# Attention scores: from two split products per head to one fp32 product of two heads side by side

## The chip, the cores and the metric

The kernel runs on one core of one Trainium2 chip. The metric is device time in microseconds (us) from the first to the last instruction of a launch, as the median over runs. Before the change it is 1330.2 us (three runs, 1329.62 to 1331.72). Engines are called as in the profile: PE is the matmul engine (PEld its weight loads), DVE the vector engine, ACT the scalar engine, POOL GpSimd, SP the engine that issues the DMAs.

## The reference

Three stages run one after the other. Shapes: q, k and v are (4, 8, 576, 64), that is 4 batches, 8 heads, 576 positions and 64 numbers per head.

```python
scores = (1.0 / np.sqrt(D)) * np.matmul(q, k.transpose(0, 1, 3, 2))
kth = np.partition(scores, -32, axis=-1)[..., -32:-31]
scores = np.where(scores >= kth, scores, -1e9)
attn = np.exp(scores - scores.max(-1, keepdims=True))
attn = attn / (attn.sum(-1, keepdims=True) + 1e-09)
x = np.matmul(attn, v)             # then heads side by side: (2304, 512)
x = ((x @ w_a) * (x @ w_b)) @ w_out
# each token goes to one of 8 experts (argmax of its cosine to expert_emb):
out[mask] = gate_w[mask, None] * (np.maximum(x[mask] @ w1[e], 0.0) @ w2[e])
```

The change touches only the first line, the scores. What is chosen after them (the 32 largest of a row, later one expert of eight) is sensitive to rounding, which is why scores are computed to fp32 precision and not in one product of rounded operands.

## The kernel before, in words

Attention works on *row tiles*: 128 query positions of one head against all 576 keys. There are 144 of them. A *part* is one pair of heads (`pr`) of a batch, and in it a share of the queries: A and B are 256 queries each, T the last 64. The list `SEQ` (0A 0BT 1A 1BT 2A 2BT 3AT 3B) gives the order of the parts, each for four pairs of heads, so 32 parts. A part has two row tiles per head, four in all, and where it has a T a fifth (kind 2), which holds 64 queries of either head. The first part of a batch and pair is its *lead*: it loads and turns the keys and stores them in DRAM, and the batch's other part reads them back.

How one row tile goes through the engines:

- **Load and split** (`load_q`, `load_k`, `split_k`, `split_qk`, L223 to L294). Raw fp32 rows of q and k are split into a rounded part (hi, type fp32r) and a rest (lo). Except for the first part, POOL does it: two instructions for the keys of a lead, three for the queries of each part. In memory a head's 64 numbers of hi and of lo lie side by side, so that 128 numbers of a position make one column to turn.
- **Turn** (`turn_qk`, L296 to L344): PE turns 128x128 blocks (L307) into PSUM, ACT copies them out (L317, L325, L331, L341). Keys: [hi | lo] over the 128 rows. Queries: twice, as [hi | lo] and as [lo | hi].
- **Scores** (`scores`, L352 to L366): for a row tile and each half of the keys (288 columns) two fp32r matmuls over all 128 rows (L364): the hi-with-hi and lo-with-lo products come out of the first, the mixed ones out of the second. ACT copies the sum to SBUF (L365). For kind 2 it is four matmuls a half, from the padded tile `qm`.
- **Top 32** (`topk`, L368): DVE takes the eight largest four times (MAX8, L385) and strikes them out between (L388).
- **Softmax** (`softmax`, L392): ACT (L397), POOL (L400), ACT (L402).
- **Turn and mix** (`turn`, `mix`, `along`, L404 to L466): PE turns the weights (L419) five blocks a row tile, ACT copies them out (L422). After the last row tile of a part PE multiplies them with the values, both heads in the two column halves of the array (L460), and spreads the sums' reciprocals (L440).

Into this stream the second stage is woven as *background*: nine groups (`moe1`, L624) of 288 fp32r matmuls of 256 columns (L683) and 72 of 512 columns (L652), with ACT and POOL work behind each, and the routing of each 128 tokens (`route`, L711).

The order is written out by hand for PE, DVE, ACT and POOL. The loop at L864 makes one *step* per row tile: `topk` of row tile `step`, softmax of `step - 2`, turning of `step - 4`, scores of `step + AHEAD_Q`, and turning of q and k from `AHEAD_P` steps ahead (`flip_next`). L946 sets the order inside a step:

```python
for slot_, g in enumerate((tg, sg, tg, mg, sg)):
    if g is not none and not run(g) and g is mg and mixes:
```

`tg` turns, `sg` is the scores, `mg` the mix of the part that has just ended. So the first half of the keys is scored between the two turnings, and the second half at the end of the step, behind the mix. Each `run` of one of them (and of each piece of `flip_next`) is followed by background worth `share`, which is the step's time budget (`STEP`, 5.4 us) less the estimated PE time of its own work, divided by the number of pieces that are expected (L935 to L945). Each engine works through its own list in order: an instruction that waits holds up all behind it. PSUM buffers of name `tr` (four) are shared by turning, scores, mix and the weights' preparation. `s` (the scores of a row tile) has `SB` buffers.

Once the last row tile is done the remaining background runs alone (L1126), and then the experts.

Of the kernel before, what the change touches and what calls it, by code (L numbers as in the profile page):

```python
# [10 lines left out]
F32 = mybir.dt.float32  # L11
# [45 lines left out]
SB = 5  # L57
# [15 lines left out]
AHEAD_P = 5  # L73
AHEAD_Q = 2
# [8 lines left out]
def fused_kernel(  # L83
# [39 lines left out]
    kT_d = drm.tile([B * NP, P, 2 * S], F32, name="kT_d")  # L123
# [74 lines left out]
    with ExitStack() as ph:  # L198
# [9 lines left out]
        qms = [wk.tile([P, 2, 2, P], F32R, name=f"qm{i}", bufs=1) for i in range(QM)]  # L208
        for t in qms:
            dve.memset(t.bitcast(F32), 0.0)  # L210
# [12 lines left out]
        def load_q(o):  # L223
            r = wk.tile([P, 5, D], F32, name="qr")
            h0 = 2 * o.pr
            for h in range(2):
                if o.M:
                    sp.dma_start(
                        r[:, 2 * h : 2 * h + 2, :].rearrange("p c d -> p (c d)"),
                        q[o.b, h0 + h, 0:512, :].rearrange("(p c) d -> p c d", c=4)[:, o.c : o.c + 2, :].rearrange(  # L230
                            "p c d -> p (c d)"
                        ),
                    )
                if o.tail:
                    sp.dma_start(r[h * 64 : (h + 1) * 64, 4, :], q[o.b, h0 + h, 512:576, :])
            return r

        def load_k(o, b, pr):
            h0 = 2 * pr
            kr = wk.tile([P, 9, D], F32, name="kr", bufs=1)  # L240
            sp.dma_start(
                kr[:, 0:8, :].rearrange("p (h c) d -> p h (c d)", h=2),
                k[b, h0 : h0 + 2, 0:512, :].rearrange("h (p c) d -> p h (c d)", c=4),
            )
            for h in range(2):
                sp.dma_start(kr[h * 64 : (h + 1) * 64, 8, :], k[b, h0 + h, 512:576, :])
            o.kr = kr

        def split_k(o):
            kr = o.kr  # L250
            ks = wk.tile([P, 9, 2, D], F32R, name="ks", bufs=1)
            if o.n:
                yield from split(ks[:, :, 0, :], ks[:, :, 1, :], kr)
            else:
                act.activation(ks[:, :, 0, :], kr, AF.Copy)
                dve.tensor_tensor(ks[:, :, 1, :], kr, ks[:, :, 0, :].bitcast(F32), op=OP.subtract)
            o.ks = ks
# [13 lines left out]
        def prep(b, pr, part, n, c0):  # L271
# [11 lines left out]
            o.qs = None  # L283
            return o

        def split_qk(o):
            qr = o.qr
            if o.lead:
                yield from split_k(o)
            qs = wk.tile([P, 5, 3, D], F32R, name="qs", bufs=1)  # L290
            js = slice(0 if o.M else 4, 5 if o.tail else 4)
            yield from split(qs[:, js, 0, :], qs[:, js, 1, :], qr[:, js])
            pool.tensor_scalar(qs[:, js, 2, :], qr[:, js], 1.0, 1.0, op0=OP.mult, op1=OP.mult)
            o.qs = qs  # L294

        def turn_qk(o):  # L296
            qs = o.qs
            o.qT = wk.tile([P, 2, 512], F32R, name="qT")
            o.kT = wk.tile([P, 2, S], F32R, name="kT", bufs=2)
            if not o.lead:  # L300
                sp.dma_start(o.kT.bitcast(F32).rearrange("p h j -> p (h j)"), kT_d[o.b * NP + o.pr])
# [4 lines left out]
            def flip(pt, c, x):  # L306
                pe.transpose(pt[:, c * P : (c + 1) * P], x.rearrange("p a d -> p (a d)"), identr)  # L307

            if o.tail:
                o.qm = qms.pop(0)  # L310
                qms.append(o.qm)
                pt = ps.tile([P, 512], F32R, name="tr", bufs=NTR)
                for a in range(2):
                    flip(pt, a, qs[:, 4, a : a + 2, :])
                qv = pt.bitcast(F32)[:, : 2 * P].rearrange("p (a h j) -> p a h j", a=2, h=2)
                for h in range(2):
                    act.activation(o.qm[:, :, h, h * 64 : (h + 1) * 64], qv[:, :, h], AF.Copy)  # L317
                yield 0.11
            if o.lead:
                for h in range(2):  # L320
                    pt = ps.tile([P, 512], F32R, name="tr", bufs=NTR)
                    for c in range(4):
                        flip(pt, c, o.ks[:, h * 4 + c])
                    if h or o.n:
                        act.activation(o.kT[:, h, 0:512], pt.bitcast(F32), AF.Copy)  # L325
                    else:
                        dve.tensor_copy(o.kT[:, h, 0:512], pt.bitcast(F32))
                    yield 0.22
                pt = ps.tile([P, 512], F32R, name="tr", bufs=NTR)
                flip(pt, 0, o.ks[:, 8])  # L330
                act.activation(  # L331
                    o.kT[:, :, 512:576], pt.bitcast(F32)[:, 0:P].rearrange("p (h j) -> p h j", h=2), AF.Copy
                )
                sp.dma_start(kT_d[o.b * NP + o.pr], o.kT.bitcast(F32).rearrange("p h j -> p (h j)"))
                yield 0.06
            for a in range(2 if o.M else 0):
# [972 lines left out]
```

## Time and profile before

| | us |
|---|---|
| median of three runs | 1330.2 |
| profiled execution | 1327.13 |
| span of its trace | 1325.2 |
| PE busy | 1181.8 (89%) |
| DVE busy | 920.5 (69%) |
| ACT busy | 820.3 (62%) |
| POOL busy | 715.1 (54%) |

The profiled execution ran 3.1 us faster than the median; its time contains 1.9 us outside of the span. The shares are averages over three quite different stages: attention with background (until about 890 us), the remaining background alone (until about 1045 us), and the experts. Busy time of PE is the union of the recorded matmuls, which overlap one another; the time from one matmul's start to the next is shorter than the duration of one. "Granted clock" is the share of the TensorE clock of 2.4 GHz that was given in a stretch; it is either 1.0 or 0.5, so that a mean between them tells how much of the stretch was at 1.2 GHz.

### The profile page before, as it was taken

To read this page: it belongs to the slowest core of one execution; us is meant where nothing else is said; L and a number is where in the kernel's file an instruction comes from. 1 tells how busy PE (TensorE), PEld (TensorE's weight loads), DVE (VectorE), ACT (ScalarE), POOL (GpSimd) and SP (SyncE) were. 2 spreads that over 40 slices of the span, in tenths; PEclk is the share of its full clock that TensorE was granted. 3 is DMA by queue.
4 is the path that set the end of the run, shared out by engine and by line. 5 is a ranking of instruction groups with operands and counts; after the bars stand their busy time and mean duration, and the time that the engine had idled before them with its cause. 6 is when DMAs were issued, how large, how long until landed. Compare 5 with 4: busy or idle time off the path is not lost. (4 is left out here: it accounts for less than half of the span.)

```text
span 1325.2 us, 23082 instructions
## 1 busy us (share of the span) xinstructions
PE 1181.8 (89%) x7828; PEld 992.9 (75%) x7829; DVE 920.5 (69%) x1991; ACT 820.3 (62%) x1953; POOL 715.1 (54%) x1160
## 2 busy tenths in 40 slices
PE   4767878987999998999999998799999989999996
PEld 3444756666888787887887787678898868888885
DVE  6989999987899988998889899750100135444440
ACT  4776888876777777776778776663532335444441
POOL 4555767755676777765767766564455321111100
PEclk9786999897999999998999999799999999999999
DMA  6333476454666666665666656457998145555520
GB/s 210 121 103 124 143 244 210 177 179 146 182 184 223 185 208 193 212 180 176 204 183 192 202 165 203 146 170 247 331 300 246 40 129 197 174 168 173 176 91 19
DMA packets 125707, 237.00 MB, mean 179 GB/s; under 512 B 22765, under 2 KB 71021, under 8 KB 125586
## 3 DMA queue, kind: packets, MB, share of 16 engines
q1 hardware_dynamic: 121426, 225.20, 53.8%
q0 software_dynamic: 4160, 10.29, 2.4%
q8 instruction: 63, 1.03, 0.3%
q14 instruction: 58, 0.48, 0.1%
HBM read 195.38 MB, written 40.85 MB: 178 GB/s over the span
## 5 line engine op out<-in xcount | busy, mean ns | idle before, releaser
L385 DVE MAX8 t<-y 128x8 f32<-128x576 f32 x432 | 312.0, 750 | 3.1
L400 POOL TENSOR_TENSOR z<-s,z 128x576 f32<-128x576 f32 x144 | 206.2, 1432 | 105.6 <-ACT z L397 103.4
L683 PE MATMUL ab<-xg,wab 128*128 128x256 f32 x1440 | 215.8, 292 | 5.6 <-ACT gab L687 3.8
L388 DVE MATCH_REPLACE8 y<-t,y 128x576 f32<-128x576 f32 x288 | 214.0, 743 | 0.0
L683 PEld LDWEIGHTS ab<-xg,wab 128*128 128x128 f32 x1440 | 190.5, 193 | 9.0 <-ACT gab L687 4.4
L683 PE MATMUL ab<-raw,wab 128*128 128x256 f32 x1152 | 173.6, 292 | 6.8 <-ACT gab L687 4.4
L419 PE MATMUL tr<-ident,z 128*128 128x128 f32 x720 | 136.0, 289 | 44.5 <-ACT z L402 36.1
L402 ACT ACTIVATE z<-z,bi 128x576 f32<-128x576 f32 x144 | 111.6, 775 | 79.5 <-POOL z L400 79.4
L683 PEld LDWEIGHTS ab<-raw,wab 128*128 128x128 f32 x1152 | 152.4, 193 | 10.8 <-ACT gab L687 5.7
L385 DVE MAX8 t<-s 128x8 f32<-128x576 f32 x144 | 107.7, 748 | 54.1 <-ACT s L365 48.8
L364 PE MATMUL tr<-kT,qT 128*128 128x288 f32 x512 | 127.8, 334 | 18.1 <-ACT s L365 13.9
L422 ACT ACTIVATE wt<-tr 128x384 f32<-128x384 f32 (+2 forms) x320 | 127.4, 413 | 17.7 <-PE tr L419 16.9
L365 ACT ACTIVATE s<-tr 128x288 f32<-128x288 f32 x288 | 118.9, 413 | 30.0 <-PE tr L364 28.6
L419 PEld LDWEIGHTS tr<-ident,z 128*128 128x128 f32 x720 | 91.6, 147 | 60.2 <-ACT z L402 39.7
L652 PE MATMUL x<-wo,gh 128*128 128x512 f32 x432 | 135.6, 395 | 0.0
L1015 DVE TENSOR_TENSOR u<-raw,u 128x1024 fp32r<-128x1024 f32 x64 | 76.2, 1221 | 83.5 <-ACT u L1014 60.6
L1064 POOL DMA_INDIRECT out_dram<-o,ids x24 | 24.0, 1000 | 200.4 <-ACT o L1063 197.1
L1092 PE MATMUL y<-u,hT 128*128 128x512 f32 (+1 forms) x528 | 128.0, 396 | 0.4 <-DVE hT L1197 0.4
L639 POOL TENSOR_TENSOR gab<-gab 128x256 f32<-128x256 f32 x108 | 81.9, 758 | 84.7 <-ACT gab L687 79.5
L364 PEld LDWEIGHTS tr<-kT,qT 128*128 128x128 f32 x512 | 89.1, 205 | 32.1 <-ACT s L365 17.5
L397 ACT ACTIVATE z<-s,bi 128x576 f32<-128x576 f32 x144 | 112.7, 783 | 0.0
L1092 PEld LDWEIGHTS y<-u,hT 128*128 128x128 f32 (+1 forms) x528 | 89.7, 173 | 27.6 <-DVE hT L1197 0.5
(178 smaller groups left out, 2211.8 us busy)
## 6 DMA issues: line engine op xcount, KB each, us to landing
wab<-wab_d SPq DMA_DIRECT2D x192, 512.0 KB
raw<-in_moe_w_dram SPq DMA_DIRECT2D x28, 1024.0 KB
wab_d<-wab SPq DMA_DIRECT2D x24, 512.0 KB
kT_d<-kT SPq DMA_DIRECT2D x16, 576.0 KB
kT<-kT_d SPq DMA_DIRECT2D x16, 576.0 KB
vs<-in_v_dram SPq DMA_DIRECT2D x32, 256.0 KB
raw<-in_moe_w_a_dram SPq DMA_DIRECT2D x12, 512.0 KB
raw<-in_moe_w_b_dram SPq DMA_DIRECT2D x12, 512.0 KB
```

The lines of the kernel that those rows point to most:

```text
L364: pe.matmul(p, l, r, start=(i == 0), stop=(i == len(terms) - 1))
L365: act.activation(t.s[:, cs], p, AF.Copy, scale=SCALE)
L385: dve.max(v, cur)
L388: dve.match_replace(out=rest, in_to_replace=v, in_values=cur, imm_value=LOWEST)
L397: act.activation(t.w, t.s, AF.Relu, bias=t.bi[:, 1:2], scale=-HUGE)
L400: pool.tensor_tensor(t.w, t.s, t.w, op=OP.subtract)
L402: act.activation(t.w, t.w, AF.Exp, bias=t.bi[:, 0:1], accum_out=t.o.sm[:, t.slot : t.slot + 1])
L419: pe.transpose(pt[:, i * P : (i + 1) * P], t.w[:, k0 : k0 + P], ident)
L422: act.activation(th[:, sl, w], pv[:, :, src], AF.Copy)
L652: pe.matmul(px[t], g[:, ts], wo[:, w, f], start=(f == 0 and i == 0), stop=(f == NF - 1 and i == 2))
L683: pe.matmul(p[:, i], wt[:, a, c, :], xg[x][:, c, :], start=(j == 0), stop=(j == len(terms) - 1))
L1092: pe.matmul(p[:m], (hi, lo)[a], u[:, b, f % 4, :], start=(f == 0 and i == 0), stop=(f == NF2 - 1 and i == 2))
```

## The change

The splits go. Raw fp32 rows of both heads are loaded side by side, so that one 128x128 block holds the 64 numbers of head 0 and the 64 of head 1, and one turning serves both heads. The scores are one fp32 matmul over 64 rows per head and half of the keys: head 0 lies in rows 0 to 63 of the array and head 1 in rows 64 to 127, and the two matmuls stand next to each other in the program with outputs in two PSUM buffers. Row tiles change their order within a part to head 0, head 1, head 0, head 1. A pair's first half of the keys is scored in one step, the second half in the next. Kind 2 becomes one fp32 matmul over 128 rows a half, with the two heads' queries on the diagonal of `qm`. The scores come three row tiles ahead instead of two, the turning six instead of five, `s` has seven buffers instead of five and `kr` two instead of one. The kept copy of the turned keys in DRAM (`kT_d`) has half the size. The loads of q and k write and read 64 numbers (256 bytes) at a time.

```diff
-SB = 5
+SB = 7
...
-AHEAD_P = 5
-AHEAD_Q = 2
+AHEAD_P = 6
+AHEAD_Q = 3
...
-    kT_d = drm.tile([B * NP, P, 2 * S], F32, name="kT_d")
+    kT_d = drm.tile([B * NP, P, S], F32, name="kT_d")
...
         def load_k(o, b, pr):
             h0 = 2 * pr
-            kr = wk.tile([P, 9, D], F32, name="kr", bufs=1)
...
+            kr = wk.tile([P, 10, D], F32, name="kr", bufs=2)
             for h in range(2):
-                sp.dma_start(kr[h * 64 : (h + 1) * 64, 8, :], k[b, h0 + h, 512:576, :])
+                sp.dma_start(
+                    kr[:, 0:8, :].rearrange("p (c h) d -> p c h d", h=2)[:, :, h],
+                    k[b, h0 + h, 0:512, :].rearrange("(p c) d -> p c d", c=4),
+                )
+            sp.dma_start(kr[0:64, 8:10, :], k[b, h0 : h0 + 2, 512:576, :].rearrange("h s d -> s h d"))
             o.kr = kr
-
-        def split_k(o):
...
-        def split_qk(o):
...
         def turn_qk(o):
...
-            def flip(pt, c, x):
-                pe.transpose(pt[:, c * P : (c + 1) * P], x.rearrange("p a d -> p (a d)"), identr)
-
+            def flip(pt, at, x):
+                n = x.shape[0]
+                pe.transpose(pt[:, at : at + n], x.rearrange("p h d -> p (h d)"), ident[:n, :n])
+
+            if o.lead:
+                pt = ps.tile([P, 512], F32, name="tr", bufs=NTR)
+                for c in range(4):
+                    flip(pt, c * P, o.kr[:, 2 * c : 2 * c + 2, :])
...
+                yield 0.43
+            pt = ps.tile([P, 512], F32, name="tr", bufs=NTR)
+            for c in range(2 if o.M else 0):
+                flip(pt, c * P, o.qr[:, 2 * c : 2 * c + 2, :])
+            if o.tail:
+                flip(pt, o.M, o.qr[0:64, 4:6, :])
+            if o.lead:
+                flip(pt, 384, o.kr[0:64, 8:10, :])
...
-        def scores(t):
-            o = t.o
-            t.s = wk.tile([P, S], F32, name="s", bufs=SB)
-            for j in range(2):
-                p = ps.tile([P, 512], F32, name="tr", bufs=NTR)[:, :288]
+        def scores(i):
+
+            kind = rows[i][5]
+            o = live[i].o
+            if kind == 2:
+                tiles, js = [live[i]], range(2)
+            elif kind == 0:
+                tiles, js = [live[i], live[i + 1]], (0,)
+            else:
+                tiles, js = [live[i - 1], live[i]], (1,)
+            for j in js:
                 cs = slice(j * 288, (j + 1) * 288)
...
+                pt = [ps.tile([P, 512], F32, name="tr", bufs=NTR)[:, :288] for _ in tiles]
+                for h, t in enumerate(tiles):
+                    if kind == 2:
+                        pe.matmul(pt[0], o.qm, o.kT[:, cs], start=True, stop=True)
+                        continue
+                    hs, ts = slice(h * 64, (h + 1) * 64), slice(t.c * P, (t.c + 1) * P)
+                    pe.matmul(pt[h], o.qT[hs, ts], o.kT[hs, cs], start=True, stop=True)
+                for t, p in zip(tiles, pt):
+                    act.activation(t.s[:, cs], p, AF.Copy, scale=SCALE)
+                yield 0.48
...
-                A, Z, T = [(0, 0, 0), (0, 1, 1)], [(1, 0, 2), (1, 1, 3)], [(2, 0, 4)]
+                A, Z, T = [(0, 0, 0), (1, 0, 2)], [(0, 1, 1), (1, 1, 3)], [(2, 0, 4)]
...
-                cost, n = cost + (0.96 if live[step + AHEAD_Q].kind == 2 else 0.48), n + 2
+                k2 = live[step + AHEAD_Q].kind == 2
+                cost, n = cost + (0.96 if k2 else 0.48), n + 1 + k2
...
             if flips:
-                cost, n = cost + 0.44, n + 2
+                cost, n = cost + 0.44, n + 1
...
-            for _ in range(2):
-                flip_next()
+            flip_next()
```

How the order of the instructions changes is shown at one place of the program, around the mix that stands at 307 us in the trace before. On PE before, L364 is scores, L307 the turning of keys (`ks`) and queries (`qs`), L419 the turning of weights, L460 and L440 the mix and its sums, L683 and L730 background:

```order
408 L364 MATMUL tr<-kT,qT 128x288 x2
409 L307 MATMUL tr<-identr,ks 128x128 x8
410 L419 MATMUL tr<-ident,z 128x128 x3
411 L683 MATMUL ab<-raw_3366,wab 128x256 x4
412 L730 MATMUL ab<-enT,x1T 128x8 x4
413 L364 MATMUL tr<-kT,qT 128x288 x2
414 L419 MATMUL tr<-ident,z 128x128 x2
415 L460 MATMUL tr<-wt,vs 64x256 x10
416 L440 MATMUL tr<-ident,rc 64x128 x4
417 L364 MATMUL tr<-kT,qT 128x288 x2
418 L307 MATMUL tr<-identr,ks 128x128
```

On PE now, around the same mix (L342 is scores, L284 the turning of keys `kr` and queries `qr`, L398 of weights, L439 and L419 the mix, L662 and L709 background):

```order
356 L284 MATMUL tr<-ident,qr 128x128 x2
357 L284 MATMUL tr<-ident,kr 128x64
358 L398 MATMUL tr<-ident,z 128x128 x3
359 L342 MATMUL tr<-kT,qT 128x288 x2
360 L662 MATMUL ab<-raw_3059,wab 128x256 x4
361 L709 MATMUL ab<-enT,x1T 128x8 x4
362 L398 MATMUL tr<-ident,z 128x128 x2
363 L439 MATMUL tr<-wt,vs 64x256 x10
364 L419 MATMUL tr<-ident,rc 64x128 x4
365 L398 MATMUL tr<-ident,z 128x128 x3
366 L662 MATMUL ab<-raw_3057,wab 128x256 x4
367 L342 MATMUL tr<-kT,qT 128x288 x2
```

The half of a row tile's scores that stood behind the mix is gone from there: a step has one pair of score matmuls, and it stands between the two turnings, ahead of the mix.

On POOL before, just ahead of that place (L218 and L220 with `ks` and `qs` and L293 are the splits, L399 and L400 the softmax, L719 to L721 routing):

```order
226 L721 TENSOR_TENSOR st<-st,tau_95 128x1
227 L218 TENSOR_SCALAR ks<-kr 128x9x64
228 L399 TENSOR_SCALAR bi<-t_3167 128x1
229 L400 TENSOR_TENSOR z<-s,z 128x576
230 L220 TENSOR_TENSOR ks<-kr,ks 128x9x64
231 L218 TENSOR_SCALAR qs<-qr 128x4x64
232 L399 TENSOR_SCALAR bi<-t_3239 128x1
233 L400 TENSOR_TENSOR z<-s,z 128x576
234 L220 TENSOR_TENSOR qs<-qr,qs 128x4x64
235 L293 TENSOR_SCALAR qs<-qr 128x4x64
236 L399 TENSOR_SCALAR bi<-t_3294 128x1
237 L400 TENSOR_TENSOR z<-s,z 128x576
```

On POOL now at the same place (L378 and L379 are the softmax, L700 routing):

```order
182 L700 TENSOR_TENSOR st<-st,tau_95 128x1
183 L378 TENSOR_SCALAR bi<-t_2877 128x1
184 L379 TENSOR_TENSOR z<-s,z 128x576
185 L378 TENSOR_SCALAR bi<-t_2936 128x1
186 L379 TENSOR_TENSOR z<-s,z 128x576
187 L378 TENSOR_SCALAR bi<-t_2988 128x1
188 L379 TENSOR_TENSOR z<-s,z 128x576
```

The five splits are gone and nothing takes their place. Over the whole program, 680 of the 2592 L683 matmuls and 186 of the 648 L652 stood behind the last turned row tile on PE before; now it is 792 and 213 of the same work (L662 and L631). The turnings of q and k fall from 432 to 160.

## Rows read from the trace of the kernel before

**Rows 1.** Busy time of the engines in three stretches (start:end, length, then engines).

```profile
18.00:300.00 282.00, 220.33 (x1253) 160.16 (x1251) 269.06 (x566) 215.27 (x498) 180.91 (x231) 0.88 0.50 167
300.00:890.00 590.00, 546.52 (x4067) 468.75 (x4068) 514.78 (x1177) 428.64 (x1115) 403.20 (x697) 0.97 0.62 186
890.00:1045.00 155.00, 146.41 (x1030) 132.85 (x1029) 16.04 (x43) 59.88 (x152) 73.02 (x152) 1.00 0.77 253
```

**Rows 2.** Waits of 300 to 890 us: waiter, awaited, us in total, times, longest.

```profile
ACT z L402 <- POOL z L400: 69.2, 53, 3.4
...
DVE t L385 <- ACT s L365: 43.5, 32, 5.1
```

**Rows 3.** Timeline of PE, 306 to 316 us: start, duration, instructions.

```profile
307.22 4.71 PE L460 MATMUL tr<-wt,vs 128*64 128x256 f32 x20
...
312.45 0.53 PE L364 MATMUL tr<-kT,qT 128*128 128x288 f32 x2
...
313.40 0.46 PE L307 MATMUL tr<-identr,qs 128*128 128x128 f32 x4
...
314.53 0.43 PE L364 MATMUL tr<-kT,qT 128*128 128x288 f32 x2
314.80 0.38 PE L419 MATMUL tr<-ident,z 128*128 128x128 f32 x2
```

**Rows 4.** Timeline of DVE in the same stretch.

```profile
313.54 0.76 DVE L385 MAX8 t<-s 128x8 f32<-128x576 f32 x1 [5.14 <-ACT s L365]
```

**Rows 5.** Busy time of the score matmuls (L364) alone, PE then PEld, same stage.

```profile
300.00:890.00 590.00, 99.50 (x440) 69.60 (x440) 0.97 0.62 186
```

**Rows 6.** Busy time of the turnings of q and k (L307) alone, same stage.

```profile
300.00:890.00 590.00, 32.73 (x273) 29.38 (x273) 0.97 0.62 186
```

**Rows 7.** Timeline of PE, matmuls of a mix (L460) around its last block.

```profile
407.14 0.71 PE L460 MATMUL tr<-wt,vs 128*64 128x320 f32 x4
...
407.41 0.86 PE L460 MATMUL tr<-wt,vs 128*64 128x320 f32 x4
...
407.78 0.76 PE L460 MATMUL tr<-wt,vs 64*64 64x320 f32 x4
...
408.10 0.44 PE L460 MATMUL tr<-wt,vs 64*64 64x320 f32 x2
```

**Rows 8.** The matmuls of that mix: ns min/median/max, first and last start, shapes.

```profile
L460 PE MATMUL tr<-wt,vs x20: 429/432/483, 405.5 to 408.1; 128*64 128x320 f32 x16, 64*64 64x320 f32 x4
```

**Rows 9.** One fp32 matmul of 512 columns over the whole array.

```profile
L550 PE MATMUL tr<-x1T,ident x2: 590/590/591, 231.5 to 231.9; 128*128 128x512 f32 x2
```

**Rows 10.** Timeline of PE, 409.2 to 412.3 us.

```profile
409.68 0.64 PE L683 MATMUL ab<-xg,wab 128*128 128x256 f32 x4
410.15 0.49 PE L419 MATMUL tr<-ident,z 128*128 128x128 f32 x3
...
411.01 0.38 PE L419 MATMUL tr<-ident,z 128*128 128x128 f32 x2
...
411.76 0.62 PE L307 MATMUL tr<-identr,qs 128*128 128x128 f32 x6
```

**Rows 11.** Timeline of PE, turnings of k and of q that waited.

```profile
301.29 1.13 PE L307 MATMUL tr<-identr,ks 128*128 128x128 f32 x8 [3.07 <-POOL ks L220]
...
834.20 1.23 PE L307 MATMUL tr<-identr,qs 128*128 128x128 f32 x8 [3.90 <-ACT wt L422]
```

**Rows 12.** Two stretches of PE: length, PE busy, granted clock, DMA share, GB/s.

```profile
301.50:311.80 10.30, 9.80 (x47) 0.50 0.19 46
830.60:844.30 13.70, 9.70 (x47) 0.50 0.15 48
```

**Rows 13.** Groups by line: the second split of the keys on POOL.

```profile
L220 POOL TENSOR_TENSOR ks<-kr,ks 128x576 fp32r<-128x576 f32 x15 | 21.6, 1440 | 0.4
```

**Rows 14.** Timeline of the program's start.

```profile
11.48 0.68 ACT L255 ACTIVATE ks<-kr 128x576 fp32r<-128x576 f32 x1
...
13.20 1.38 PE L307 MATMUL tr<-identr,ks 128*128 128x128 f32 x9 [13.20 <-DVE ks L256]
```

More of the change, by code (lines that the diff above doesn't have):

```diff
@@ L206, in fused_kernel @@
         sp.dma_start(ids_d.rearrange("(p r) c -> p (r c)", p=P), fill)
-        qms = [wk.tile([P, 2, 2, P], F32R, name=f"qm{i}", bufs=1) for i in range(QM)]
+        qms = [wk.tile([P, P], F32, name=f"qm{i}", bufs=1) for i in range(QM)]
         for t in qms:
-            dve.memset(t.bitcast(F32), 0.0)
+            dve.memset(t, 0.0)
         zrow = mk.tile([P, RW], F32, name="xr")
@@ L223, in load_q @@
         def load_q(o):
[L224 removed]
+            r = wk.tile([P, 6, D], F32, name="qr")
             h0 = 2 * o.pr
[L226 to L227 removed]
+            if o.M:
+                for h in range(2):
                     sp.dma_start(
[L229 to L232, printed above, removed]
[L233 to L235 removed]
+                        r[:, 0:4, :].rearrange("p (c h) d -> p c h d", h=2)[:, :, h],
+                        q[o.b, h0 + h, 0:512, :].rearrange("(p c) d -> p c d", c=4)[:, o.c : o.c + 2],
+                    )
+            if o.tail:
+                sp.dma_start(r[0:64, 4:6, :], q[o.b, h0 : h0 + 2, 512:576, :].rearrange("h s d -> s h d"))
             return r
@@ L282, in prep @@
             o.qr = load_q(o)
-            o.qs = None
             return o
-        def split_qk(o):
[L287 to L294, printed above, removed]
         def turn_qk(o):
-            qs = o.qs
-            o.qT = wk.tile([P, 2, 512], F32R, name="qT")
-            o.kT = wk.tile([P, 2, S], F32R, name="kT", bufs=2)
+            o.qT = wk.tile([P, 320], F32, name="qT")
+            o.kT = wk.tile([P, S], F32, name="kT", bufs=2)
             if not o.lead:
-                sp.dma_start(o.kT.bitcast(F32).rearrange("p h j -> p (h j)"), kT_d[o.b * NP + o.pr])
+                sp.dma_start(o.kT, kT_d[o.b * NP + o.pr])
             o.wt = [None, None]
@@ L861, in fused_kernel @@
         thresholds = [none]
-        coming = []
         soft = none
@@ L919, in fused_kernel @@
                 en_turn(mp, e_sb)
-            for o in coming[:1]:
-                if step >= o.first - AHEAD_P or (step >= o.first - AHEAD_P - 2 and not flips):
-                    pieces.append(split_qk(o))
-                    coming.pop(0)
-                    while step < EAGER and pieces:
-                        piece()
             while 0 <= step + AHEAD_Q < NRW and live[step + AHEAD_Q].o in flips:
@@ L933, in fused_kernel @@
             tg = turn(live[i]) if 0 <= i < NRW else none
-            sg = scores(live[step + AHEAD_Q]) if 0 <= step + AHEAD_Q < NRW else none
+            sg = scores(step + AHEAD_Q) if 0 <= step + AHEAD_Q < NRW else none
             mg = mixes[0] if mixes else none
```

72 lines of the change are left out of this document (16 added, 56 removed).

## Prediction

> **What bounds the kernel now.** I read the busy time by stretches first, then the waits of the middle stretch, then the timeline where the longest waits stand.
>
> In the first stretch, 18 to 300 us, DVE is busy 269 of 282 us and PE 220 [rows 1]: the top-32 search sets the pace, and PE work that is added there costs nothing. In the middle, 300 to 890 us, PE is busy 546.5 of 590 us and DVE 514.8. Neither is full, and each idles because of the other: DVE waited 43.5 us, 32 times, for scores [rows 2], and PE was idle 590 - 546.5 = 43.5 us for many small reasons. From 890 to 1045 us only the background is left, and PE is busy 146 of 155 us. PE is thus the engine to count in the last two stretches: a matmul that goes from the one to the other costs the same in both, and what the program gains is PE work removed after 300 us, plus PE idle time removed there.
>
> One long wait shows how the stage goes wrong. The mix began at 307.22 and took 4.71 us; the scores that DVE needed stood behind it in PE's list and began at 312.45 [rows 3], and DVE sat idle for 5.14 us until 313.54 [rows 4]. In the order before, the second half of a row tile's scores (L364) is the entry behind L460 and L440; in the new order nothing of the scores stands there.
>
> **The change part by part, against the profiled execution of 1327.1 us** (3.1 us under the median; I carry the sum over to 1330.2).
>
> *Scores on PE.* The middle stretch holds 440 of the old matmuls [rows 5]: 86 row tiles of four and 12 tails of eight. Two of them take 0.27 us from their start to the start of the next instruction (314.53 to 314.80) [rows 3], so 0.135 us each and 59 us in all. The new ones are fp32 over half the rows, which the trace does not show. The nearest thing is the mix: fp32 matmuls in the two column halves, one head in each. The program has 10 of them and the trace 20 [rows 8], so an fp32 matmul is two passes. Four such instructions of 320 columns take 0.71 us and two alone 0.44 [rows 7], so a couple adds 0.27 us. Over the whole array a 512-column pass adds about 0.4 us (231.5 to 231.9) [rows 9], 0.25 us per 320 columns. A couple in two column halves therefore costs what one pass costs, and the halves run together. If row halves do the same, a pair of score matmuls is two couples of 288 columns, 2 x 0.27 x 288/320 = 0.49 us. If they do not, it is 0.97.
>
> To that comes the change of the array's shape. In the same mix the last block uses 64 rows instead of 128: couples start at 407.14, 407.41, 407.78 and 408.10, so the change made two gaps of 0.27 into 0.37 and 0.32 [rows 7], 0.15 us. A pair of scores goes in and out of the half-row shape, so 0.30 us. I take 0.49 + 0.30 = 0.79 us for a pair, and the middle stretch has 86 pairs (one per row tile, since a pair does half of the keys for two): 68 us. The 24 tail matmuls over the full array are 0.49 each, 12 us. Together 80 us against 59: **+21 us**. Ends: 0.49 (no cost of the change) gives -5, 0.97 + 0.30 gives +62. The value chosen stands on the nearest row, the mix, which has halves, fp32 and the change of rows in one place.
>
> The Trainium skill ("TensorEngine Tiling (Array Packing)", Tiling Modes, Key Properties) says that switching the tiling mode drains the engine, while another tile of the same mode does not. It speaks against weaving one small pair at a time into full-array work, and the 0.27 that became 0.37 agrees with it. Without the rule the term would be -5; with it, +21. The same skill ("TensorE: Matmul & The Clock Gate", Part 3, Measured speedup vs the span model) gives 3.07 for four row tiles. As an estimate from that page, 77% of the ideal on two halves would make the pair 0.63 instead of 0.49 and the term +33. No run here shows it yet.
>
> *Turning q and k on PE.* 273 turnings in the middle stretch [rows 6]. Six take 0.62 us [rows 10] and four 0.46 [rows 3], so 0.08 each and 22 us. Now there are 160/432 of them, 101, in plain fp32: three take 0.49 and two 0.38 [rows 10], 0.11 each, 11 us, and some 20 use 64 rows and pay up to 0.30 for the shape, 6 us. **-5 us** (-11 to 0).
>
> *Splits on POOL.* They were late twice: turnings of keys waited 3.07 us for the second split and turnings of queries 3.90 us [rows 11]. The second is put down to an ACT copy; what it turns (`qs`) comes from POOL's splits, so I count it to them. Both go: **-7 us** (-3 if the second is ACT's). Around both PE ran 10.3 and 13.7 us at a granted clock of 0.50, that is 1.2 GHz [rows 12], after it had been idle. That costs half of 24 us. Other waits share in the cause, so I take half of the 12: **-6 us** (-12 to 0).
>
> *The rest of PE's idle time.* 43.5 less 7 leaves 36 us. ACT stood still 69.2 us, 53 times, for POOL's softmax subtraction [rows 2], and behind it in ACT's list wait the copies that free PE's buffers. POOL loses the splits (one of five groups alone is 21.6 us [rows 13]), the scores no longer stand behind the mix, and they come up to one row tile earlier, with seven buffers. Against that, the score pair takes two of the four PSUM buffers at once. I take a quarter, **-9 us** (0 to -30).
>
> *Start.* The split of the first keys began at 11.48 and the turning at 13.20 [rows 14]. With no split, and fewer copies behind, DVE starts about **-2.5 us** earlier (-4 to +1; the low side because q and k now arrive in 256-byte pieces). DVE sets the pace there, so it carries through.
>
> *The moved background.* 112 of the L683 (0.47 us for four, 409.68 to 410.15 [rows 10], so 0.12 each) and 27 of the L652 (some 0.23 each, in proportion to the columns) pass behind the last row tile: 13.4 + 6.2 = 20 us. They leave the middle stretch and lengthen the next: nothing, as long as PE sets the pace of both. If DVE does, the 20 us are lost. Of the ACT copies and the DMAs that go (half of each kept key tile) I count nothing more: ACT is busy 429 of 590 us and the DMA share is 0.62 [rows 1].
>
> Sum: 21 - 5 - 7 - 6 - 9 - 2.5 = -8.5 us. From 1330.2: **1322 us**.
>
> **Rivals.**
>
> *The row halves do not overlap, or only in part* (ends slower; in this the change does not do what it says). Place: each of the 86 pairs. At 0.97 + 0.30 the sum is -8.5 + 41 = +33, 1363 us. If the second pass of head 0 must finish before head 1 begins its second, a pair takes three passes, 0.73 + 0.30: +12, 1343 us. For it: no row shows two row halves. Against it: column halves overlap [rows 7]. It decides from a pair of about 0.92 us on, where the sum turns to slower. Chance 0.20; 1350 between the two.
>
> *DVE sets the pace of the middle stretch* (ends level or slower). PE's relief then shortens the stretch only by waits that DVE loses, while the 20 us of moved background come on top behind it. Place: 890 to 1045 us. If DVE loses a third of its 43.5 us, 15: -2.5 - 15 + 20 = +2, 1333 us. For it: DVE is busy 514.8 of 590 with nothing taken from it. Against it: its waits end when PE delivers. Chance 0.17.
>
> *The waits nearly all go* (faster). PE's idle time falls by 28 instead of 9 of its 36 us: -8.5 - 19 = -27.5, 1303 us. For it: the longest DVE wait stands behind a mix, and that place is emptied. Against it: PE's idle time has many small reasons, of which scores are one. Chance 0.13.
>
> **How the numbers follow.** My forecast has 0.50: 1322 us, alone 1308 to 1336, by the terms' own bounds. About what can be told from no change is 0.2%, 2.7 us. Faster than that: 0.50 x 0.70, all of the third rival, a fifth of the second, together 0.52. Within: 0.50 x 0.14 and a third of the second, 0.12. Slower: the first rival, half of the second and the rest, 0.36. The range reaches just past the third rival's value below and to the first's full price above: 1302 to 1363.
>
> **What would show it.** In the changed profile: a pair of score matmuls in the row halves takes about 0.5 us from the first start to the second couple's end of streaming, with gaps of some 0.1 us going in and coming out; four instructions start two by two. L342's busy time in the whole program tells the rest. DVE's waits for scores fall below 25 us, and none of 3 us or more stands behind a mix. No turning waits for POOL. The last row tile ends some 28 us earlier (8.5 + 20), and the background alone takes some 20 us longer than before. The forecast is wrong if the four instructions start one by one, if gaps around a pair are well over 0.3 us, or if the attention stretch does not shorten while the next lengthens.

## The result, and the profile after

The changed kernel takes **1340.2 us** (median of six, 1334.4 to 1342.5) against 1329.9 on the same chip: ratio 1.0066, 95% interval 1.0038 to 1.0093. It is slower by 0.7%; the forecast was 1322 us, faster, so its sign was wrong. The range held the time. The profiled execution took 1342.5 us, its span is 1340.1.

Busy time by stretches answers [rows 1]: start:end, length, PE, PEld, DVE, ACT and POOL busy with counts, granted clock, DMA share, GB/s. Attention now ends near 880 us and the background near 1057, so these two stretches are shown besides.

```profile
18.00:300.00 282.00, 223.48 (x1154) 134.76 (x1151) 264.07 (x569) 208.51 (x489) 152.70 (x188) 0.87 0.48 155
300.00:890.00 590.00, 555.76 (x3782) 423.34 (x3783) 509.23 (x1173) 401.64 (x1077) 351.81 (x610) 0.96 0.59 171
890.00:1045.00 155.00, 142.83 (x996) 129.94 (x995) 13.39 (x34) 51.71 (x136) 71.83 (x148) 1.00 0.87 268
```

```profile
300.00:880.00 580.00, 545.76 (x3705) 415.24 (x3706) 508.71 (x1169) 398.03 (x1068) 346.85 (x599) 0.96 0.59 172
880.00:1057.00 177.00, 164.12 (x1142) 147.44 (x1141) 15.66 (x42) 60.27 (x155) 80.73 (x167) 1.00 0.79 243
```

From 300 us to the end of the background (1045 before, 1057 now) PE was busy 546.5 + 146.4 = 692.9 us and idle 52.1 [rows 1]; now it is busy 545.8 + 164.1 = 709.9 and idle 47.1. PE is busy 17 us longer there and idle only 5 us less: 9 less in attention (34.2 instead of 43.5) and 4 more behind it (12.9 instead of 8.6). Of its busy time 41 us now passed at 1.2 GHz, against 32 before, so by estimate some 4 of the 17 us are the clock and 13 are work. By the last turning of weights attention ended at 895.5 us before and at 880.2 now, 15 us earlier and not the forecast 28; the background behind it took 176.5 us instead of 147.1, 29 longer and not 20.

The waits of 300 to 890 us (waiter, awaited, us in total, times, longest) answer [rows 2]:

```profile
ACT z L381 <- POOL z L379: 130.1, 77, 3.6
DVE m L716 <- ACT lg L712: 41.9, 7, 9.0
PE tr L439 <- ACT wt L401: 9.6, 9, 2.5
DVE t L364 <- ACT s L344: 7.3, 6, 2.5
...
PE tr L284 <- ACT wt L401: 4.5, 3, 3.9
PE tr L419 <- ACT wt L401: 3.3, 2, 2.0
```

DVE's waits for scores fell from 43.5 to 7.3 us, as hoped. But ACT's waits for POOL's subtraction (L379) nearly doubled, from 69.2 to 130.1, although POOL lost the splits and is busy 352 instead of 403 us. DVE's waits for the routing (L716) rose too, from 15.5. And PE now waits for ACT's copies of turned weights (L401) in the mix (L439), the sums (L419) and the turnings of q and k (L284).

One such wait, on POOL, ACT and PE of the changed kernel (start, duration, instruction, in brackets the idle time before it and what ended it):

```profile
798.31 1.41 POOL L379 TENSOR_TENSOR z<-s,z 128x576 f32<-128x576 f32 x1
```

```profile
795.10 0.77 ACT L376 ACTIVATE z<-s,bi 128x576 f32<-128x576 f32 x1
795.77 0.37 ACT L401 ACTIVATE wt<-tr 128x256 f32<-128x256 f32 x1
799.76 0.77 ACT L381 ACTIVATE z<-z,bi 128x576 f32<-128x576 f32 x1 [3.62 <-POOL z L379]
800.44 0.19 ACT L381 ACTIVATION_READ_ACCUMULATOR z<-z,bi 128x1 f32 x1
800.53 0.47 ACT L401 ACTIVATE wt<-tr 128x384 f32<-128x384 f32 x1
```

```profile
796.02 0.49 PE L398 MATMUL tr<-ident,z 128*128 128x128 f32 x3
796.44 0.76 PE L342 MATMUL tr<-kT,qT 64*128 64x288 f32 x4
797.12 0.74 PE L662 MATMUL ab<-raw,wab 128*128 128x256 f32 x4
797.70 0.38 PE L398 MATMUL tr<-ident,z 128*128 128x128 f32 x2
...
801.06 0.88 PE L439 MATMUL tr<-wt,vs 128*64 128x320 f32 x4 [2.50 <-ACT wt L401]
```

ACT's next entry is the exponential (L381); it stands for 3.62 us. Behind it in the list is the copy of three turned blocks, ready since 796.5, and PE's mix cannot begin before that copy is done. POOL was late here although its input had come from ACT by 795.9: in its list the subtraction stood behind routing instructions (L729 to L743), one of which had waited 1.29 us for a DMA. The clock fell to half, 1.2 GHz, half a microsecond after this wait of PE, and likewise near the end of one of 3.94 us for such a copy, until 765.16 (a turning of q, L284):

```profile
764.00:774.20 10.20, 9.04 (x33) 6.16 (x35) 8.73 (x21) 7.20 (x18) 4.50 (x7) 0.50 0.08 20
801.60:805.00 3.40, 3.40 (x14) 1.22 (x10) 3.37 (x9) 1.25 (x4) 2.28 (x3) 0.50 0.00 0
```

Why this copy? The step's PE work takes the four `tr` buffers in turn. Before, that was first turning, scores, second turning, mix: the mix took the fourth. Now the pair of scores takes two, so the mix is fifth and takes the buffer of the step's own first turning, whose copy stands behind the exponential. That is read from the code; a fifth buffer was not tried, but run 1 frees one buffer and bears it out.

The pair of scores on PE:

```profile
502.09 0.40 PE L631 MATMUL x<-wo,gh 128*128 128x512 f32 x1
502.42 0.51 PE L342 MATMUL tr<-kT,qT 64*128 64x288 f32 x2
...
502.77 0.41 PE L342 MATMUL tr<-kT,qT 64*128 64x288 f32 x2
503.11 0.33 PE L398 MATMUL tr<-ident,z 128*128 128x128 f32 x1
```

They start two by two, 0.35 us apart, and the next instruction starts 0.69 us after the first. So row halves do run together, and the first rival is out. The next start does not tell the whole price, because the instruction behind is held up too. Over the 32 visits after 300 us that stand between background matmuls (L662) at the full clock, the time from the start of the matmul ahead to the start of the third behind, less three usual gaps of 0.119, is 0.88 us.

### The profile page after: what moved, and what is told of

Its sections match the earlier page's. It is cut to its first block, busy times and chain, and to the rows that moved or that the text cites. A ratio compares the mean times of both kernels' runs of the same rounds, so it can differ in the third digit from the quotient of the medians.

```text
span 1340.1 us, 22093 instructions
## 1 busy us (share of the span) xinstructions
PE 1206.2 (90%) x7492; PEld 930.1 (69%) x7493; DVE 908.9 (68%) x1989; ACT 784.8 (59%) x1905; POOL 636.5 (47%) x1034
## 5 line engine op out<-in xcount | busy, mean ns | idle before, releaser
L364 DVE MAX8 t<-y 128x8 f32<-128x576 f32 x432 | 312.0, 750 | 3.0
L379 POOL TENSOR_TENSOR z<-s,z 128x576 f32<-128x576 f32 x144 | 206.7, 1436 | 135.0 <-ACT z L376 130.2
L662 PE MATMUL ab<-xg,wab 128*128 128x256 f32 x1440 | 213.4, 293 | 7.0 <-DMA wab<-wab_d 3.4
L662 PEld LDWEIGHTS ab<-xg,wab 128*128 128x128 f32 x1440 | 187.2, 193 | 26.7 <-issue 13.2
L381 ACT ACTIVATE z<-z,bi 128x576 f32<-128x576 f32 x144 | 111.3, 773 | 147.5 <-POOL z L379 147.3
L662 PE MATMUL ab<-raw,wab 128*128 128x256 f32 x1152 | 175.0, 295 | 8.2 <-DMA wab<-wab_d 6.7
L398 PE MATMUL tr<-ident,z 128*128 128x128 f32 x720 | 137.5, 293 | 47.7 <-ACT z L381 41.6
L662 PEld LDWEIGHTS ab<-raw,wab 128*128 128x128 f32 x1152 | 150.3, 192 | 26.0 <-issue 14.7
L398 PEld LDWEIGHTS tr<-ident,z 128*128 128x128 f32 x720 | 88.9, 148 | 86.1 <-ACT z L381 49.2
L631 PE MATMUL x<-wo,gh 128*128 128x512 f32 x432 | 136.3, 397 | 0.0
L401 ACT ACTIVATE wt<-tr 128x384 f32<-128x384 f32 (+2 forms) x320 | 126.4, 407 | 14.8 <-PE tr L398 14.2
L618 POOL TENSOR_TENSOR gl<-gab,gh 128x256 fp32r<-128x256 f32 x108 | 81.8, 758 | 71.2 <-ACT gh L618 62.7
L364 DVE MAX8 t<-s 128x8 f32<-128x576 f32 x144 | 107.0, 743 | 10.1 <-ACT s L344 10.1
L344 ACT ACTIVATE s<-tr 128x288 f32<-128x288 f32 x288 | 103.8, 411 | 17.0 <-PE tr L342 14.0
L342 PE MATMUL tr<-kT,qT 64*128 64x288 f32 x512 | 108.0, 491 | 2.3 <-ACT wt L401 1.8
```

Source lines behind the costliest of these rows:

```text
L342: pe.matmul(pt[h], o.qT[hs, ts], o.kT[hs, cs], start=True, stop=True)
L364: dve.max(v, cur)
L379: pool.tensor_tensor(t.w, t.s, t.w, op=OP.subtract)
L381: act.activation(t.w, t.w, AF.Exp, bias=t.bi[:, 0:1], accum_out=t.o.sm[:, t.slot : t.slot + 1])
L398: pe.transpose(pt[:, i * P : (i + 1) * P], t.w[:, k0 : k0 + P], ident)
L401: act.activation(th[:, sl, w], pv[:, :, src], AF.Copy)
```

## The experiments

Each ran against the kernel before on the same chip; ratios are to it, with 95% intervals. Medians of different chips differ by a few us, so gains between two runs are worked out from their ratios (0.01 is 13.3 us). Theory 1, from the first comparison: PE sets the pace, and the change of shape around each pair ate the gain.

**1. No change of shape.**

```diff
-pt = [ps.tile([P, 512], F32, ...)[:, :288] for _ in tiles]
+pt = [ps.tile([P, 512], F32, ...)[:, :288]] * len(tiles)
...
-pe.matmul(pt[h], o.qT[hs, ts], o.kT[hs, cs], start=True, stop=True)
+if h == 0: pe.matmul(pt[0], o.qT[:, ts], o.kT[:, cs], start=True, stop=True)
```

> The changed kernel, but each pair of score matmuls is one fp32 matmul over all 128 rows whose sum both row tiles copy. Left out: the separate scores of the two heads. Copies, order, buffers and budgets stay; the streaming stays too (two passes of 288 columns, 0.49 us), only the change of the array's shape goes. Theory 1 (PE sets the pace from 300 us on, and the change of shape around each pair, about 0.37 us by the changed kernel's trace, is what ate the gain): 128 visits x 0.37 = 47 us less PE work in the program, 86 x 0.37 = 32 us of it after 300 us, so 1340 - 32 = about 1308 us, 1300 to 1320. Rival A (the deeper lookahead and DVE's waits for the routing cost the time) and rival B (background that moved behind the last row tile is the loss): PE's work in the attention stretch is not what counts, so 1335 to 1342 us.

Measured: 1319.2 us, 0.9940 (0.9917 to 0.9964), 17 us less than the changed kernel (1.0066 - 0.9940), short of 32. PE work counts, but not in full.

```profile
499.64 0.65 PE L343 MATMUL tr<-kT,qT 128*128 128x288 f32 x2
499.92 0.85 PE L663 MATMUL ab<-xg,wab 128*128 128x256 f32 x4
500.60 0.40 PE L632 MATMUL x<-wo,gl 128*128 128x512 f32 x1
```

The next start comes 0.28 us after the first, but the four background matmuls there are held: from 499.64 to 500.60 it is 0.96 us, and four of them take 4 x 0.12 = 0.48, so the visit costs 0.48 to 0.49 us (0.49 over 31 visits, measured as above) instead of 0.88. The dose was 0.39 x 86 = 34 us.

The expectation says that the buffers stay, but they do not: the pair's one sum takes one of the four `tr` buffers, so the mix is fourth again and the sums are fifth. The waits moved with it (300 to 890 us; L420 is the sums, L440 the mix):

```profile
PE tr L420 <- ACT wt L402: 6.7, 7, 2.1
...
PE tr L440 <- ACT wt L402: 3.0, 3, 1.7
```

The mix's fell from 9.6 to 3.0 us and the sums' rose from 3.3 to 6.7, as the order of the buffers has it. The 17 us are therefore not the price of PE work alone; run 10 repeats the dose without these waits.

**2. Both halves of the keys in one visit.**

```diff
-tiles, js = [live[i], live[i + 1]], (0,)
+tiles, js = [live[i], live[i + 1]], (0, 1)
```

> The changed kernel with all four matmuls pairs of two row tiles in one go: both halves of the keys for both heads, so half as many visits to the half-row shape (64 instead of 128), at the price of all four PSUM buffers at once; the pieces are paced so that 120 of the 792 background matmuls that were left behind the last row tile go back into attention. Theory 1: 43 visits fewer after 300 us x 0.37 = 16 us, so about 1324 us (1318 to 1330); a wait for PSUM buffers in each group may take some of it back. Rival B: the 15 us of background that goes back into attention is hidden there, which alone gives 1325; told apart by the run with the longer step. Rival A: no change, 1338 to 1342.

Measured: 1343.4 us, 1.0119 (1.0097 to 1.0142), a miss. Taking all four buffers at once made a wait of its own, so what the fewer visits gave can't be read from this run:

```profile
PE tr L344 <- ACT wt L406: 18.7, 23, 3.8
```

**3. The old lookahead** (`SB` 7 to 6, `AHEAD_Q` 3 to 2).

> The changed kernel with the lookahead of the scores put back to two row tiles and six score buffers. Theory 1: PE's work is the same, and which wait stands ends up the same, so 1340 us within 4. Rival A (the deeper lookahead turned DVE's waits for scores into waits for the routing, and these cost the time): DVE's waits for the routing fall from 42 to about 16 us and the kernel gains up to 10 us, 1330. If instead the lookahead was worth what the prediction hoped, it gets slower by 5 to 10 us, 1345 to 1350, with DVE waiting for scores.

Measured: 1353.2 us, 1.0192 (1.0167 to 1.0216). Rival A is out: the deeper lookahead, with its buffer, is worth 17 us. DVE's waits for the routing did fall, from 41.9 to 27.9 us, but it waits for scores again:

```profile
DVE t L364 <- ACT s L344: 49.9, 32, 6.7
```

**4. The background back in its place** (`STEP` 5.4 to 5.7).

> The changed kernel with the step's time budget at 5.7 instead of 5.4 us, which leaves 680 + 186 background matmuls behind the last row tile, as before the change, instead of 792 + 213. Theory 1: PE's work only goes from one stretch into the other, 1340 us within 4; if the idle time at the tail (4 to 10 us for weights from DRAM) falls back too, up to 5 us faster. Rival B (DVE sets the pace of attention, so that background moved behind it is lost): the 20 us are hidden again, 1320 to 1325 us.

Measured: 1322.5 us, 0.9965 (0.9939 to 0.9990). Theory 1 fails: the 20 us of moved background cost 13.

**5. The same background moved in the kernel before** (`STEP` 5.4 to 5.1), and as a control the longer step there (5.4 to 5.7).

> The kernel before with the step's time budget at 5.1 instead of 5.4 us, which leaves exactly as much background behind the last row tile as the changed kernel does: 792 + 213 matmuls instead of 680 + 186, 20 us more. Nothing else is touched. Theory 2, formed on the run of the changed kernel with the longer step (1322.5 against 1340 us): attention is paced by DVE and the chain around it and has room for this background, so what is left behind it is lost; 12 to 18 us slower than before, 1339 to 1345. Theory 1 (PE sets the pace of both stretches, work only moves): 1327 within 4.

> The kernel before with the step's budget at 5.7 instead of 5.4 us: 672 + 186 matmuls are left, about as many as it has anyway. It tells whether the longer step is a gain in itself. Theory 3 (what counts is how much background is left): 1328 within 4. If the longer step spaces PE's list better whatever is left: 1318 to 1323, and the changed kernel's gain with that step is not the change's.

Measured: 1343.2 us, 1.0100 (1.0071 to 1.0130), and 1327.4 us, 1.0007 (0.9986 to 1.0029). So moved background costs some 13 us there too, and a longer step that moves nothing gains nothing.

**6. Less work on DVE.**

```diff
+if t.n >= 48 and t.n % 4 == 0 and r == 2:
+    t.thr = t8[:, 23:24]
+    break
```

> The changed kernel with the last round of the top-32 search (one strike-out of 0.74 us and one MAX8 of 0.75) left out for every fourth row tile from the 48th on, whose threshold is then the 24th largest: 24 x 1.49 = 36 us less DVE work, all after 300 us. Theory 2 (DVE paces the attention): 20 to 36 us faster than the changed kernel, 1304 to 1320. Theory 1 (PE paces it): no gain, 1336 to 1342. The run without the change of shape took 32 us of PE work away after 300 us and gained 21; if both doses gain about 20, the two engines pace the stretch by turns, each waiting for the other.

Measured: 1341.1 us, 1.0089 (1.0063 to 1.0115): no gain from 36 us. DVE's waits for scores rose from 7.3 to 19.3 us instead. DVE does not set the pace, and theory 2 fails with its mechanism, though its numbers had come true in runs 4 and 5.

**7. The splits back on POOL**, unread.

```diff
+yield from split(qs[:, :, 0, :], qs[:, :, 1, :], o.qr[:, 0:4])
+pool.tensor_scalar(qs[:, :, 2, :], o.qr[:, 0:4], 1.0, 1.0, op0=OP.mult, op1=OP.mult)
```

> The changed kernel with the old splits put back on POOL as work that nobody reads: per lead two instructions over 8 x 64 numbers, per part three over 4 x 64. If POOL's relief was worth what the prediction gave it (7 us for the splits' waits, and a share of the 9 for PE's other idle time): 1345 to 1352 us. If the waits behind POOL's softmax subtraction are off the path, as theories 1 and 2 have it: 1340 within 4, although ACT's waits for POOL grow by some 50 us.

Measured: 1352.0 us, 1.0176 (1.0150 to 1.0203). POOL's relief is worth 15 us in this kernel. By which way is shown only in part: 4 us are lost by row tile 24, whose search starts at 168.0 us instead of 163.6; between 300 and 890 us ACT's waits for POOL rose by 9 us, not 50 (139.1 against 130.1), the mix's from 9.6 to 12.3, and PE was idle 6 us more (40.5 against 34.2).

**8. Still more background in attention** (`STEP` 6.0, `DEBT` 2.0).

> The changed kernel with a step budget of 6.0 us and a cap of 2.0 instead of 1.0 us on what one piece may owe, which leaves 604 + 168 background matmuls behind the last row tile: 76 x 0.12 + 18 x 0.23 = 13 us less than the run with the 5.7 us step (1322.5). Theory 2: most of it is hidden too, 8 to 11 us faster than that run, about 1312 to 1315. Theory 1, or if PE has become the bound of attention once the 20 us are back: 1322 within 4, or slower, because longer runs of background delay the turnings and scores.

Measured: 1346.8 us, 1.0142 (1.0113 to 1.0171), 24 us more than run 4, where theory 2 expected less. More background was used before 700 us (1440 + 351 matmuls against 1392 + 332); from 700 to 860 PE had 295 + 81 against 437 + 112, and its granted clock was 0.86 instead of 0.99. The budget and the cap were changed together, so which of them did it stays open. Run 4 and this one, 700 to 860 us:

```profile
700.00:860.00 160.00, 149.92 (x1043) 115.08 (x1041) 143.68 (x331) 110.26 (x300) 98.83 (x186) 0.99 0.60 182
```

```profile
700.00:860.00 160.00, 137.34 (x835) 98.77 (x834) 133.84 (x305) 100.63 (x268) 83.71 (x151) 0.86 0.46 140
```

**9. The exponential one place later in ACT's list.** Theory 3: background had covered the place where PE waits for ACT, and ACT for POOL. From step 20 on (POOL's addition to the row sums, which reads its result, goes with it):

```diff
-next(soft, None)
+late = soft if step >= 20 else none
...
+if slot_ == 0 and step >= 20:
+    next(late, None)
```

> The changed kernel with one place in ACT's list changed, from step 20 on: the softmax's exponential (L381), which waits for POOL's subtraction, goes behind the first copy of turned weights (L401) of the step instead of ahead of it. Background and budgets are the changed kernel's (792 + 213 left). Theory 3: the moved background cost 15 to 18 us because it had covered the places where PE waits for ACT's copies, and ACT stands there behind the exponential that waits for POOL (120.8 us, 73 times between 300 and 850 us; PE's waits for those copies some 20 us). Then ACT's waits for POOL fall below 80 us, PE's for the copies below 10, and the kernel gains 8 to 15 us: 1325 to 1332. If these waits are only where the idle time shows and not why it is there, they move to another place: 1340 within 4.

> The same later place of the exponential, with the 5.7 us step that leaves 680 + 186 background matmuls as before. Theory 3: the two cures overlap, so less than their sum: 3 to 8 us below the run with the 5.7 us step alone (1322.5), 1314 to 1319. Otherwise 1322 within 4.

Measured: **1304.7 us**, 0.9837 (0.9806 to 0.9868), and with the longer step 1305.4 us, 0.9845 (0.9807 to 0.9883). One place in a list gives 30 us, where 8 to 15 were expected, and with it the moved background costs nothing. Waits of the first, 300 to 890 us, and its ACT around one exponential:

```profile
ACT z L381 <- POOL z L379: 79.7, 61, 2.8
...
PE tr L284 <- ACT wt L401: 0.4, 2, 0.2
PE tr L439 <- ACT wt L401: 0.3, 1, 0.3
```

```profile
503.75 0.49 ACT L401 ACTIVATE wt<-tr 128x384 f32<-128x384 f32 x1 [0.74 <-PE tr L398]
505.52 0.78 ACT L381 ACTIVATE z<-z,bi 128x576 f32<-128x576 f32 x1 [1.28 <-POOL z L379]
```

ACT still waits for POOL, but the copy is ahead of the wait, and PE's waits for it are gone. PE's account from 300 us is now:

```profile
300.00:844.00 544.00, 527.66 (x3684) 404.68 (x3681) 503.80 (x1159) 395.54 (x1058) 342.83 (x596) 0.99 0.61 181
844.00:1019.00 175.00, 165.15 (x1145) 149.74 (x1143) 15.93 (x42) 59.58 (x156) 80.40 (x167) 0.98 0.77 245
```

Idle 719 - 692.8 = 26.2 us, 21 less than in the changed kernel, and busy 17 less for the same work, 10 of them by estimate the clock: 20 us of its busy time passed at 1.2 GHz instead of 41.

**10. Which engine sets the pace then.** Runs 1 and 6 again, with the later exponential.

> The changed kernel with the later exponential, and each pair of score matmuls as one fp32 matmul over all 128 rows whose sum both row tiles copy (left out: the separate scores of the two heads). With the old place the 32 us of PE work after 300 us that this takes away gained 21. If PE alone sets the pace once ACT's list is mended (theory 1 at last): 25 to 32 us below 1304.7, 1273 to 1280. If DVE takes over (it is busy 504 of 560 us by now): 10 to 20 us, 1285 to 1295.

> The changed kernel with the later exponential and 36 us less DVE work after 300 us (the last round of the search left out for every fourth row tile from the 48th on). With the old place it gained nothing. PE sets the pace: 1304.7 within 4. DVE sets it: 1270 to 1290.

Measured: 1283.1 us, 0.9648 (0.9620 to 0.9677), 25 us for the PE dose of 34, and 1311.3 us, 0.9848 (0.9813 to 0.9882), nothing for the DVE dose. The mix's waits for copies are 0.3 and 0.5 us in the two kernels of the PE dose, so here the buffers play no part. PE sets the pace, most of the way.

**11. The later exponential in the kernel before**, with its own and with the moved background.

> The kernel before with the exponential behind the first copy of turned weights in ACT's list from step 20 on, as in the run of the changed kernel that gained 35 us. Theory 3 with the stall in both kernels: before, ACT waits half as long for POOL there (62 against 121 us between 300 and 850), so it gains about half, 1308 to 1318, and with ACT's list mended the changed kernel is 5 to 15 us faster than the one before, as the prediction's sum had it. Rival: the stall is of the change's own making (the row tiles' new order and the scores' new place in ACT's list), then before gains nothing: 1324 to 1330.

> The same, with the step's budget at 5.1 us, which leaves 792 + 213 background matmuls. With the old place of the exponential these 20 us cost 15. Theory 3 (background that is moved is lost only where it had covered that wait): the run above within 4 us, as the changed kernel showed it (1304.7 with 792 + 213, 1305.4 with 680 + 186). Rival (moved background is lost in the kernel before for another reason): 10 to 15 us slower than the run above.

Measured: 1331.3 us, 1.0011 (0.9988 to 1.0034), and 1340.8 us, 1.0085 (1.0056 to 1.0114). The expected half gain did not come; the rival holds: what the changed kernel loses there came with the change. Moved background still costs 10 us there, so another wait loses it in that kernel; which one stays open.

**12. One part of the change alone:** in the kernel before, the scores' second half ahead of the mix; then with the later exponential too.

```diff
-for slot_, g in enumerate((tg, sg, tg, mg, sg)):
+for slot_, g in enumerate((tg, sg, tg, sg, mg)):
```

> The kernel before with the second half of each row tile's scores ahead of the mix instead of behind it: the one part of the change that empties the end of a step. In ACT's list the second score copy then no longer stands between the softmax's mask (L397) and its exponential (L402). Theory 3: ACT's wait for POOL's subtraction rises from 69 us towards the changed kernel's 130 (300 to 890 us), above 100, and 5 to 15 us are lost, 1333 to 1343, although DVE's long waits behind the mix (43.5 us in all) get fewer. The prediction's view (scores out from behind the mix help): 1318 to 1325.

> The same, with the exponential also behind the step's first copy of turned weights. Theory 3: the loss is given back and the scores' earlier place shows its worth, 5 to 15 us faster than the run above and at most 1328. If the later place helps only together with the fp32 scores and the row tiles' new order: no difference from the run above.

Measured: 1338.7 us, 1.0118 (1.0091 to 1.0145), and **1294.3 us**, 0.9768 (0.9752 to 0.9784), far past the expected 5 to 15 us. Waits of the first, then of the second:

```profile
ACT z L402 <- POOL z L400: 94.5, 64, 4.1
...
PE tr L460 <- ACT wt L422: 22.1, 18, 3.3
```

```profile
ACT z L402 <- POOL z L400: 31.9, 38, 2.7
...
DVE t L385 <- ACT s L365: 15.4, 20, 2.9
```

The new order alone brings the mix's wait for the copy (22.1 us), lets ACT's waits for POOL rise from 69.2 to 94.5 us, a little less than expected, and loses 16 us; with the copy ahead of the exponential that wait is gone, and the order is worth 31 us. This version, still with split scores, beats both kernels. With 680 + 186 matmuls left in both, the one with fp32 scores (run 9, longer step) stands at 0.9845 against 0.9768: the rest of the change costs 0.8%, some 10 us.

**13. The 256-byte pieces** in the kernel before (loads of q and k).

> The kernel before with q and k loaded in 256-byte pieces as the changed kernel loads them (places in the tiles permuted, the rest as it was). The rival that small pieces slow the transfers: the first search starts up to 1 us later and the weights that the second stage reads arrive late, 1332 to 1338. All three theories: no effect, 1328 within 4.

Measured: 1328.7 us, 1.0010 (0.9989 to 1.0032). They cost nothing.

## Why the prediction was wrong

- **The rest of PE's idle time** (-9, and -7 for the splits' waits) is the step that failed. PE's idle time fell by 5 us, not 16. The prediction read the 69.2 us of ACT's waits for POOL and expected them to shrink with POOL's work; they rose to 130.1. It did name the pair's two PSUM buffers as a point against, but did not follow which buffer the mix would get. The Trainium skill ("TensorEngine Tiling (Array Packing)", Gotcha 1: PSUM Pressure) says that row tiles write to different PSUM banks and so raise the pressure on PSUM. The mix's wait of 2.50 us above is such pressure in this case; who would wait, and for what, the page does not say. The wait that should have been priced is the mix's, for a copy behind the exponential. Run 9 shows the price of that place in ACT's list, 30 us; run 12 that the wait came with the order.
- **Half clock** (-6) failed with it: new waits took the place of the old. The stretches at 1.2 GHz after 300 us add up to 44 us instead of 38, about +4 us. In the profiled executions the kernel lost 15.4 us (1327.1 to 1342.5) where the sum had -8.5; of these 24 us, the idle time is 11 and the clock 10.
- **The moved background** (0) also hung on that wait. It held "as long as PE sets the pace of both": run 10 shows PE does, most of the way, once ACT's list is mended, and run 9 then shows the moved background free. With the stall in place it cost 13 (run 4). Its size was short as well: alone it takes not 20 us but 26 to 28, from the last turning of weights to the last background matmul (run 4 against the changed kernel 150.3 and 176.5 us; the two of run 9, 146.4 and 174.0). Why is not shown. The rival that DVE sets the pace gave 1333; its mechanism is refuted by run 6.
- **Scores on PE** (+21) **and turning** (-5): their sum of +16 was about right, 13 to 17 by PE's busy time, but not its parts. The pair was priced at 0.79 us, 0.49 for streaming and 0.30 for the shape; it takes 0.88, and run 1 shows the 0.49 without the change of shape, so the shape costs 0.39 and the term comes to 87 - 59 = +28. The turnings must then have given back more than 5: their own busy time fell from 32.7 [rows 6] to 17.1 us. That two misses cancel is luck. A change of the array's shape costs, as the Trainium skill has it ("TensorEngine Tiling (Array Packing)", Tiling Modes, Key Properties). Going in, the trace agrees: the pair's first start comes 0.21 us behind the start of a background matmul, where 0.12 is usual.
- **Splits off POOL**: no turning waits for POOL any more, and putting the splits back costs 15 us (run 7). That run has the stall in it; what the relief would be worth without the stall was not run.
- **Start** (-2.5): the right way and half the size. The first search started at 16.85 us instead of 18.00, and at row tile 24 the search starts at 163.6 instead of 165.2.
- Of the three rivals, the time that is reached without the stall, 1304.7, is near that of "the waits nearly all go" (1303), but in another kernel, so it is no test of that rival. That the first rival's middle case gave 1343, near the time measured, is chance: its condition, head 1 behind head 0's second pass, did not come.

## What to carry to other kernels

When entries move in one engine's list, follow the buffers that rotate under them: a fifth user of four buffers waits for whatever stands ahead of the first user's copy. Look in the copying engine's list for an instruction that waits for a third engine, and put the copies ahead of it. It pays only where a buffer waits for such a copy: the same later exponential gained nothing in the kernel before (run 11) and 30 us in the changed one. And background that moves out of a stretch can cost time if it had covered such a wait there (13 us here with the wait, nothing without it); a budget that brings it back is a quick test.

## What the runs showed of the hardware

Two fp32 matmuls in the two row halves ran as one: the four instructions of a pair start in two couples 0.35 us apart. In the longer visits of run 2 the third couple started 0.24 us behind the second, as the second pass behind the first in a full-array matmul of the same columns (run 1, 0.245). A visit of one pair between full-array matmuls cost 0.88 us of PE (changed kernel, 32 visits), against 0.49 for one fp32 matmul over the full array (run 1, 31 visits); the difference is the change of shape. The start of the next instruction came after 0.69 and 0.28 us and tells less than the whole, since that instruction was held up.
